# A decode kernel: the first weight load cut into 16 and 112 partitions

## The chip, the cores and the metric

The kernel runs on one core of one Trainium2 chip. The metric is the device time of the whole program in microseconds (us); lower is better.

## The reference

One decode step: a layernorm of x, attention over a cache of 32768 positions with 32 heads, and a SwiGLU feed-forward, both added to x.

```python
D = 640; Hq = Hkv = 32; Sk = 32768; Dh = 128; F = 1728          # all bf16, one token
xn = layernorm(x)
q = (xn @ wq).reshape(32, 128)                                   # wq: 640 x 4096, 5.2 MB
scores = einsum("hd,hkd->hk", q, k_cache) * Dh ** -0.5           # k_cache: 32 x 32768 x 128
o = einsum("hk,hkd->hd", softmax(scores), v_cache)               # v_cache: the same size
out = x + o.reshape(4096) @ wo + (silu(xn @ w_gate) * (xn @ w_up)) @ w_down
```

K and V are 537 of the 554 MB that are read.

## The kernel before

SBUF is the core's on-chip memory, which the kernel uses as 128 rows, called partitions. PE is the matrix engine, DVE the vector engine and ACT the scalar engine; SP only issues loads here. SBUF holds a ring of three slots of 64 KB per partition. The loads take the slots in the order wq, K of head 0, K of head 1, V of head 0, K of head 2 and so on; each waits until what its slot held has been used. They are all issued from SP, on one DMA queue. wq and x are issued at the very start of the program, ahead of the barrier that lets the engines begin.

```python
units = [("wq",)]
for h in range(H):
    units.append(("k", h))
    if h >= 1:
        units.append(("v", h - 1))
...
ring = sbt("ring", [128, SLOTS, CE], BF16)              # CE = 32768 elements
wq = flat[:, WQ_S * CE:WQ_S * CE + NCD * H * DH]        # 128 partitions x 20480 elements = 40 KB each
...
ahead(lambda: nc.sync.dma_start(wq, A_wq.rearrange("(p c) n -> p (c n)", c=NCD)).then_inc(s_wq, 16))
ahead(lambda: nc.scalar.dma_start(xrow, A_x[0, 0:1, :]).then_inc(s_x, 16))
...
# SP, for each unit in turn
if s in owner:
    e.wait_ge(*owner.pop(s))                            # the slot's last user is done
...
elif u[0] == "k":
    e.dma_start(ring[:, s, :], kv_src(A_k_cache, u[1], 0, NJ)).then_inc(s_slot[s], 16)
...
# PE: q = xn @ wq, after the layernorm and after wq has landed
t.wait_ge(s_a, 11)
t.wait_ge(s_wq, 16)
with t.Fori(0, NQB) as b:
    for c in range(NCD):
        mm = t.matmul(banks[:, bass.ds(b * 512, 512)], lhsT=xnb[:, c, :],
                      rhs=wq[:, bass.ds(b * 512 + c * H * DH, 512)], ...)
```

For each head DVE multiplies K by q, PE sums the products, ACT takes the exponentials, and PE multiplies by V.

Of the kernel before, what the change touches and what calls it, by code (L numbers as in the profile page):

```python
# [12 lines left out]
def bass_parallel_sum__gqa_block_cached__swiglu_ffn__decode_kernel(  # L13
# [18 lines left out]
    NCD = D // 128  # L32
# [47 lines left out]
    with ExitStack() as es:  # L80
# [3 lines left out]
        def sem(name):  # L84
            return es.enter_context(nc.semaphore(name))
# [34 lines left out]
        s_x, s_wq, s_out = sem("x"), sem("wq"), sem("o")  # L120
# [18 lines left out]
        wq = flat[:, WQ_S * CE:WQ_S * CE + NCD * H * DH]  # L139
# [7 lines left out]
        def ahead(start):  # L147

            at_start = nc.main_func.blocks[0]
            n = len(at_start.instructions)  # L150
            start()
            ins = list(at_start.instructions)
            new = ins[n:]
            drain = next(i for i, x in enumerate(ins)
                         if x.engine == new[0].engine and type(x).__name__ == "InstDrain")
            at_start.instructions = ins[:drain] + new + ins[drain:n]

        ahead(lambda: nc.sync.dma_start(wq, A_wq.rearrange("(p c) n -> p (c n)", c=NCD)).then_inc(s_wq, 16))
        ahead(lambda: nc.scalar.dma_start(xrow, A_x[0, 0:1, :]).then_inc(s_x, 16))
        block = es.enter_context(nc.Block(no_gpsimd_drain=True))  # L160
        f0 = FFN_S * CE
# [46 lines left out]
        with nc.psum_tensor("ps8", [128, 8, 512], F32) as ps8:  # L208
# [72 lines left out]
            def pe(t):  # L281
# [13 lines left out]
                t.matmul(misc[:, 1:2], lhsT=ones[:, :], rhs=st[:, 2:3], start=True, stop=True).then_inc(s_pa, 1)  # L295

                t.wait_ge(s_a, 11)
                t.wait_ge(s_wq, 16)
                with t.Fori(0, NQB) as b:
                    for c in range(NCD):  # L300
                        mm = t.matmul(banks[:, bass.ds(b * 512, 512)], lhsT=xnb[:, c, :],  # L301
# [373 lines left out]
```

## Time and profile before

| | before |
|---|---|
| time, median | 1286.4 us (1286.2 to 1286.6) |
| bytes moved, mean rate | 554 MB, 431 GB/s |
| DMA, PE, DVE busy | 99.8%, 81%, 52% |
| wq, from issue to landing | 15.0 us |
| first DVE multiply of head 0 starts | 34.5 us |

Lines of the profile's page before the change. The DMA and GB/s rows cut the span into 40 slices of 32 us; a 9 is a busy share of 90% or more of the 16 DMA engines. The last line sums the chain of work that ended last.

```profile
span 1284.8 us, 10032 instructions
...
DMA  9999999999999999999999999999999999999998
GB/s 424 424 453 425 426 427 445 428 433 441 431 433 426 445 428 433 439 433 426 433 445 428 431 431 441 428 433 445 428 431 426 445 428 433 439 433 431 428 429 368
DMA packets 10987, 554.16 MB, mean 431 GB/s; under 512 B 1247, under 2 KB 1504, under 8 KB 1760
...
q1 hardware_dynamic: 10974, 554.00, 99.8%
...
DMA 53%; PE 29%; DVE 11%; issue 6%; DVEq 0%; SPq 0%
```

The DMA engines have work in every slice, so the kernel is bound by its stream of loads.

The timeline of the kernel before (start, duration, engine, line, operation; in brackets the idle time before it and what ended it):

```profile
0.00 0.41 SPq L158 DMA_DIRECT2D ring<-in_A_wq_dram  x1
...
1.76 0.35 PE L286 MATMUL ps<-one,ring 1*128 1x1 bf16 x5 [1.76 <-DMA ring<-in_A_x_dram]
...
15.41 11.10 PE L301 MATMUL ps<-ring 128*128 x40 [10.60 <-DMA ring<-in_A_wq_dram]
...
34.50 17.43 DVE L577 TENSOR_TENSOR ring<-ring,qb 128x8192 bf16<-128x8192 bf16 x4 [27.80 <-DMA ring<-in_A_k_cache_dram]
```

wq is the first thing that PE needs after the layernorm: it waits 10.6 us for it. DVE then waits for K of head 0, the next load in the queue.

The DMA issues of the kernel before (times issued, KB if one size, median us from issue to landing):

```profile
ring<-in_A_wq_dram SPq DMA_DIRECT2D x1, 5120.0 KB, 15.0
...
ring<-in_A_k_cache_dram SPq DMA_DIRECT2D x32, 41.4
```

A K load takes 41.4 us from issue to landing, though 8.4 MB at 433 GB/s need 19.4 us: about two loads are queued at any time.

Windows of the kernel before; the last two columns are DMA share and GB/s (bytes are counted where a packet starts, so short windows are rough):

```profile
core 0: us, PE busy (x) PEld busy (x) DVE busy (x) ACT busy (x) POOL busy (x), PEclk, DMA share, GB/s
0.00:15.00 15.00, 1.66 (x14) 1.40 (x14) 2.55 (x13) 1.49 (x2) 2.61 (x18) 1.00 1.01 420
15.00:30.00 15.00, 11.10 (x40) 4.48 (x40) 0.00 (x0) 6.06 (x9) 0.00 (x0) 1.00 0.97 419
30.00:45.00 15.00, 5.93 (x17) 0.20 (x2) 10.50 (x3) 0.00 (x0) 0.00 (x0) 0.54 0.97 419
...
100.00:1200.00 1100.00, 908.89 (x4043) 210.39 (x2309) 596.41 (x345) 39.44 (x112) 0.00 (x0) 0.90 1.00 434
```

The trace also records each DMA packet. In wq's load a packet is one partition's 40 KB row. The records do not name the engine, but the packets follow one another in 16 chains of eight, one chain for each DMA engine. Sorted by start and taken in rounds of 16, their median durations in ns are:

```
kernel before: 2140 1514 1514 1514 1514 1514 1514 1514   last wq packet ends at 14.69 us
```

Apart from the start-up in the first, a packet takes 1.514 us: 27.05 GB/s per engine, 433 GB/s for 16. The first packet starts at 1.02 us. Each chain ends with one packet of 4 bytes, 16 in all, of 9 ns each: as many as the load adds to its semaphore, the completion writes.

### The profile page before, as it was taken

What the parts mean: (1) busy time and instruction counts of PE and PEld (TensorE: products, weight loads), DVE (VectorE), ACT (ScalarE), POOL (GpSimd) and SP (SyncE); (2) the same over time, 40 slices, a digit from 0 to 9 for tenths busy, and PEclk for the clock granted to TensorE, in tenths of its full rate; (3) what the DMA queues carried; (4) which work ended last, traced back from release to release, by engine and by line L of the source; (5) the groups of instructions that cost most, each with busy time, mean ns of one, the idle gap of its engine ahead of it and who ended that gap; (6) DMA issues with size and microseconds to landing.
All of it is one profiled execution on the core that took longest, in us unless ns stands there. A gap on an engine that the chain in (4) does not pass through costs nothing.

```text
span 1284.8 us, 10032 instructions
## 1 busy us (share of the span) xinstructions
PE 1043.2 (81%) x5160; PEld 261.3 (20%) x3240; DVE 672.2 (52%) x409; ACT 52.2 (4%) x139; POOL 2.6 (0%) x18
## 2 busy tenths in 40 slices
PE   3599777789777788778898887798788798778897
PEld 1021112221112221112221112221112221112227
DVE  0855665445664446664446664446654446654451
ACT  2000000000000000000000000000000000000000
POOL 0000000000000000000000000000000000000000
PEclk9799888898888999888998888998888998888995
DMA  9999999999999999999999999999999999999998
GB/s 424 424 453 425 426 427 445 428 433 441 431 433 426 445 428 433 439 433 426 433 445 428 431 431 441 428 433 445 428 431 426 445 428 433 439 433 431 428 429 368
DMA packets 10987, 554.16 MB, mean 431 GB/s; under 512 B 1247, under 2 KB 1504, under 8 KB 1760
## 3 DMA queue, kind: packets, MB, share of 16 engines
q1 hardware_dynamic: 10974, 554.00, 99.8%
q8 instruction: 9, 0.15, 0.0%
q14 instruction: 2, 0.02, 0.0%
q10 hardware_dynamic: 2, 0.00, 0.0%
HBM read 553.99 MB, written 0.00 MB: 431 GB/s over the span
## 4 chain that ended last, share of the span: by engine, by line
DMA 53%; PE 29%; DVE 11%; issue 6%; DVEq 0%; SPq 0%
DMA ring<-in_A_k_cache_dram 51%; PE ps L358 16%; DVE ring L577 11%; PE ps L310 10%; DMA ring<-in_A_wo_dram 2%; PE ps L342 1%; PE ps L329 1%; PE ps L400 0%; PE ps L394 0%; PE ps L388 0%; PE ps L451 0%; SPq L252 0%; DVEq L577 0%; DVE sc L583 0%; DVE pmax L589 0%
## 5 line engine op out<-in xcount | busy, mean ns | idle before, releaser
L577 DVE TENSOR_TENSOR ring<-ring,qb 128x8192 bf16<-128x8192 bf16 x128 | 557.8, 4420 | 314.8 <-DMA ring<-in_A_k_cache_dram 314.8
L310 PE MATMUL ps<-ring,ident 128*128 128x512 bf16 x1920 | 498.9, 419 | 0.0
L358 PE MATMUL ps<-ring,P 128*4 128x512 bf16 x1920 | 429.0, 379 | 0.0
L329 PE MATMUL ps<-ring,ident 128*128 128x512 bf16 x128 | 55.9, 437 | 218.7 <-DVE ring L577 218.2
L358 PEld LDWEIGHTS ps<-ring,P 128*4 128x4 bf16 x1920 | 158.1, 85 | 230.1
L329 PEld LDWEIGHTS ps<-ring,ident 128*128 128x128 bf16 x128 | 12.6, 99 | 616.9 <-issue 313.3
L583 DVE TENSOR_REDUCE sc<-ps 128x64 f32<-128x512 f32 x128 | 82.3, 684 | 63.8 <-PE ps L310 63.8
L595 DVE TENSOR_SCALAR negb<-ps 128x1 f32<-128x1 f32 x32 | 5.1, 159 | 108.4 <-PE ps L400 108.4
L503 ACT ACTIVATE P<-sc,negb 128x256 bf16<-128x256 f32 x32 | 16.2, 508 | 956.9 <-DVE negb L595 956.9
L592 DVE TENSOR_REDUCE m<-ps 1x1 f32<-1x128 f32 x32 | 8.9, 278 | 85.2 <-PE ps L394 85.2
L380 PEld LDWEIGHTS ps<-identf,o 4*128 4x128 f32 x248 | 30.7, 190 | 13.1 <-issue 13.1
L380 PE MATMUL ps<-identf,o 4*128 4x1 f32 x248 | 33.3, 251 | 0.0
L388 PEld LDWEIGHTS ps<-rsum,ones 128*128 128x128 f32 x64 | 12.1, 190 | 99.9 <-issue 99.1
L494 ACT ACTIVATE o<-ps,rzb 4x512 f32<-4x512 f32 x31 | 21.0, 678 | 6.3 <-PE ps L345 6.3
L301 PE MATMUL ps<-ring 128*128 x40 | 11.1, 448 | 10.6 <-DMA ring<-in_A_wq_dram 10.6
L499 ACT ACTIVATE ocol<-ps 128x1 f32 (+1 forms) x31 | 5.4, 174 | 222.3 <-PE ps L380 222.3
L342 PE MATMUL ps<-ring,P 128*4 x64 | 14.4, 379 | 0.0
L589 DVE TENSOR_REDUCE pmax<-sc 128x1 f32<-128x256 f32 x32 | 13.4, 420 | 0.0
L394 PE MATMUL ps<-identf,pmax 128*1 128x128 f32 x64 | 12.2, 272 | 1.2 <-DVE pmax L589 1.2
L400 PE MATMUL ps<-m,ones 1*128 1x1 f32 x64 | 12.1, 256 | 0.4 <-DVE m L592 0.4
L400 PEld LDWEIGHTS ps<-m,ones 1*128 1x128 f32 x64 | 9.4, 182 | 14.0 <-issue 13.3
L565 DVE RECIPROCAL rzb<-ps 128x1 f32<-128x1 f32 x32 | 5.1, 158 | 8.1 <-PE ps L388 8.1
(75 smaller groups left out, 97.4 us busy)
## 6 DMA issues: line engine op xcount, KB each, us to landing
ring<-in_A_v_cache_dram SPq DMA_DIRECT2D x2, 4096.0 KB, 36.3
ring<-in_A_wq_dram SPq DMA_DIRECT2D x1, 5120.0 KB, 15.0
ring<-in_A_wo_dram SPq DMA_DIRECT2D x3, 1280.0 KB, 24.2
ring<-in_B_w_gate_dram SPq DMA_DIRECT2D x1, 2160.0 KB, 22.6
ring<-in_B_w_up_dram SPq DMA_DIRECT2D x1, 2160.0 KB, 27.5
ring<-in_B_w_down_dram SPq DMA_DIRECT2D x1, 2080.0 KB, 30.9
ring<-in_A_wo_dram SPq DMA_DIRECT2D x1, 800.0 KB, 28.3
ring<-in_A_k_cache_dram SPq DMA_DIRECT2D x32, 41.4
```

The source lines that it names most:

```text
L310: return t.add_instruction(mybir.InstMatmult(start_tensor_calc=False, stop_tensor_calc=stop, tile_size=(128, 128), tile_position=(0, 0), l ...
L329: t.matmul(ob, lhsT=ident[:, :], rhs=src, start=True, stop=False)
L342: t.matmul(O, lhsT=P[:, h % PR, bass.ds(b * (RUN * W) + j, W)], rhs=flat[:, bass.ds(b * (RUN * W * DH) + (s * CE + j * DH), W * DH)], star ...
L358: mm = t.matmul(O, lhsT=P[:, h % PR, j:j + W], rhs=ring[:, s, j * DH:(j + W) * DH], start=(j == 0), stop=(j + W == NJ))
L380: mm = t.matmul(fold_ps, lhsT=o4[:, m * DH:(m + 1) * DH], rhs=identf[0:W, m:m + 1], start=(m == 0), stop=(m == W - 1))
L394: t.matmul(misc[0:1, 0:128], lhsT=pmax[:, h % SR:h % SR + 1], rhs=identf[:, :], start=True, stop=True).then_inc(s_t, 1)
L400: t.matmul(misc[:, 128:129], lhsT=ones[0:1, :], rhs=m1[0:1, h % SR:h % SR + 1], start=True, stop=True).then_inc(s_b, 1)
L494: a.activation(out=o4[:, :], in_=O, func=ACTF.Copy, scale=rzb[0:W, h % SR:h % SR + 1]).then_inc(s_o4, 1)
L503: a.activation(out=P[:, h % PR, :], in_=sc[:, :], func=ACTF.Exp, bias=negb[:, h % SR:h % SR + 1], scale=c_scale, accum_out=rsum[:, h % SR: ...
L577: v.tensor_tensor(out=kh, in0=kh, in1=q[:, None, :].to_broadcast([128, HF, DH]), op=ALU.mult).then_inc(s_mul, 1)
L583: v.tensor_reduce(out=sc[:, i * HF:(i + 1) * HF], in_=bank[i].rearrange("p (j e) -> p j e", e=G), axis=AX.X, op=ALU.add).then_inc(s_red, 1)
L589: v.tensor_reduce(out=pmax[:, h % SR:h % SR + 1], in_=sc[:, :], axis=AX.X, op=ALU.max).then_inc(s_max, 1)
```

## The change

The first load is cut in two, 16 partitions (one 40 KB packet for each of the 16 chains) and then the other 112. The natural intent is that a small first load is set up sooner, so that the engines start sooner. Both loads count on the same semaphore, and PE waits for both.

```diff
-        ahead(lambda: nc.sync.dma_start(wq, A_wq.rearrange("(p c) n -> p (c n)", c=NCD)).then_inc(s_wq, 16))
+        wq_src = A_wq.rearrange("(p c) n -> p (c n)", c=NCD)
+        for a, b in ((0, 16), (16, 128)):
+            ahead(lambda: nc.sync.dma_start(wq[a:b, :], wq_src[a:b, :]).then_inc(s_wq, 16))
...
-                t.wait_ge(s_wq, 16)
+                t.wait_ge(s_wq, 32)
```

## The prediction

> **What bounds the kernel now.** The stream of loads. The page gives 554.16 MB at a mean of 431 GB/s over a span of 1284.8 us, the DMA row shows 9 in every slice until the last, and queue 1's packets fill 99.8% of the 16 engines' time. The chain of waits is mostly K-cache loads (51%), and PE or DVE work in it overlaps queued transfers: a K load takes a median 41.4 us from issue to landing, about two 8 MB transfers (19.3 us each at 433 GB/s), so the queue is never empty. Hence whatever delays the slowest DMA engine at the start comes back nearly 1:1 in the total.
>
> **The start, from the timeline and DMA windows.** wq's issue takes 0.41 us on SP; the first bytes move at about 1.0 us; wq (128 rows of 40 KB, eight per engine) lands 15.0 us after issue. The layernorm chain is done at 6.7 us, so the q matmuls wait 10.6 us for wq. They end near 26.5 us; K of head 0 lands at 34.4 us, so wq may land some 8 us later before q delays the first DVE multiply.
>
> **What the change does.** Same bytes, same queue. It adds one issue (0.41 us on SP, hidden: 5 MB are queued behind it) and 16 completion writes (nanoseconds each). The intended gain is an earlier first byte. The small x load, issued at 0.12 us, also starts moving near 1.0 us (0.9 us later), so at most 0.1-0.2 us can be gained: 0.01%.
>
> **The possible cost.** [...] The present trace, with 128-partition loads only, can't tell. [...] I worked an estimate [...] from 27 GB/s per engine (433/16) and contiguous groups of seven: wq lands near 23-26 us instead of 15, fast engines running ahead into K, and the slowest engine ends 10 us late. That delay persists to the end.
>
> If the 112 were dealt round robin[...]: about +36 us (estimate, same sharing). [...]
>
> **Predicted time:** 1295 us, that is +8.5 us (0.7%); 8 in 10 between 1286 and 1300. Chances: faster by over 2% 0.01, within 2% 0.89, slower by over 2% 0.10.
>
> **What would show each step.**
> - First byte still near 1.0 us (windows at the start).
> - Crowding: GB/s in the first slice of the page falls from 424 while the DMA share stays at 9; the wq issues' time to landing rises to 23-26 us; the first DVE multiply starts near 44 us rather than 34.5.
> - From the third slice on, GB/s as before (425-453), and per-head spacing unchanged at some 38.7 us; all the difference lies before 50 us and shifts everything after.
>
> **What would make it wrong.** [...] Round robin dealing: then 1322. A lag that is partly recovered because engines end unequal and the last transfers even them out: then +3 to +6 us.

The forecast's sum came to 1295 us: 1286.4 of the kernel before and 8.5 for the change. 23 to 26 us for wq, 10 us for the slowest engine and +36 us (1322) for dealing round robin were estimates. The completion writes that it names took 9 ns each in the trace before, and 13 to 41 ns each for the two loads of the change.

## The result

The changed kernel took 1298.78 us (median of four, 1298.68 to 1299.03) against 1286.36 us: 12.4 us or 1.0% slower. The ratio is 1.0097 (95% interval 1.0079 to 1.0114); ratios are the mean time of one kernel's fast runs over that of the other's of the same rounds, so not quite the ratio of the medians quoted.

The page after the change:

```profile
span 1297.3 us, 10033 instructions
...
DMA  9999999999999999999999999999999999999998
GB/s 259 449 423 437 433 427 439 428 441 428 430 438 428 445 424 430 438 428 445 428 430 436 432 438 428 436 432 430 438 428 438 430 430 438 428 441 428 430 428 362
DMA packets 11004, 554.17 MB, mean 427 GB/s; under 512 B 1263, under 2 KB 1520, under 8 KB 1776
...
q1 hardware_dynamic: 10990, 554.00, 99.7%
...
DMA 53%; PE 28%; DVE 12%; issue 6%; DVEq 0%; SPq 0%
```

The first slice fell from 424 to 259 GB/s while the DMA row stayed at 9: the engines are as busy as before and move less. 165 GB/s less over 32.4 us (1297.3 / 40) is 5.3 MB, which at 431 GB/s is 12.4 us: the whole loss stands in that one slice. From the third slice on the rates are those of before.

The timeline after:

```profile
0.00 0.86 SPq L160 DMA_DIRECT2D ring<-in_A_wq_dram  x2
...
2.82 0.35 PE L288 MATMUL ps<-one,ring 1*128 1x1 bf16 x5 [2.82 <-DMA ring<-in_A_x_dram]
...
27.87 11.01 PE L303 MATMUL ps<-ring 128*128 x40 [22.00 <-DMA ring<-in_A_wq_dram]
...
46.97 17.43 DVE L579 TENSOR_TENSOR ring<-ring,qb 128x8192 bf16<-128x8192 bf16 x4 [39.21 <-DMA ring<-in_A_k_cache_dram]
```

q's matmuls start 12.46 us later (27.87 against 15.41), the first DVE multiply 12.47 us later (46.97 against 34.50). The layernorm started about 1 us later too, behind the x load (2.82 against 1.76), without effect: PE still waited 22 us for wq.

The issues and windows after:

```profile
ring<-in_A_wq_dram SPq DMA_DIRECT2D x1, 4480.0 KB, 27.0
...
ring<-in_A_wq_dram SPq DMA_DIRECT2D x1, 640.0 KB, 8.8
ring<-in_A_k_cache_dram SPq DMA_DIRECT2D x32, 41.5
```

```profile
core 0: us, PE busy (x) PEld busy (x) DVE busy (x) ACT busy (x) POOL busy (x), PEclk, DMA share, GB/s
0.00:15.00 15.00, 1.66 (x14) 1.41 (x14) 2.55 (x13) 1.49 (x2) 2.59 (x18) 1.00 1.02 205
15.00:30.00 15.00, 2.13 (x6) 0.84 (x7) 0.00 (x0) 0.00 (x0) 0.00 (x0) 1.00 0.94 285
30.00:45.00 15.00, 8.88 (x36) 3.60 (x34) 0.00 (x0) 6.06 (x9) 0.00 (x0) 0.92 1.03 446
...
100.00:1200.00 1100.00, 902.05 (x4031) 211.71 (x2327) 593.55 (x339) 40.30 (x115) 0.00 (x0) 0.90 1.00 434
```

The 16 partitions took 8.8 us to land; the 112 took 27.0. Between 100 and 1200 us both kernels move 434 GB/s, and the median K or V packet takes 2.422 us in both. The packets of wq, as above:

```
kernel after: 4810 3790 2884 2180 2368 2573 2785 2630   last wq packet ends at 26.73 us
```

No packet of the changed load took less than 1.84 us, where nearly all took 1.51 before. The last one ends 12.0 us later, which is nearly all of the 12.4 us. The first packet starts at 1.03 us, so the intended gain is not there at all.

### The profile page after: what moved, and what is told of

It reads as the page before. It is cut to its first block, busy times and chain, and to the rows that moved or that the text cites. A ratio compares the mean times of both kernels' runs of the same rounds, so it can differ in the third digit from the quotient of the medians.

```text
span 1297.3 us, 10033 instructions
## 1 busy us (share of the span) xinstructions
PE 1038.6 (80%) x5160; PEld 261.3 (20%) x3240; DVE 672.2 (52%) x409; ACT 52.1 (4%) x139; POOL 2.6 (0%) x18
## 4 chain that ended last, share of the span: by engine, by line
DMA 53%; PE 28%; DVE 12%; issue 6%; DVEq 0%; SPq 0%
DMA ring<-in_A_k_cache_dram 51%; PE ps L360 16%; DVE ring L579 12%; PE ps L312 9%; DMA ring<-in_A_wo_dram 2%; PE ps L344 1%; PE ps L331 1%; PE ps L402 0%; PE ps L396 0%; PE ps L390 0%; PE ps L453 0%; SPq L254 0%; DVEq L579 0%; DVE sc L585 0%; DVE pmax L591 0%
## 5 line engine op out<-in xcount | busy, mean ns | idle before, releaser
L312 PE MATMUL ps<-ring,ident 128*128 128x512 bf16 x1920 | 493.0, 415 | 0.0
L331 PE MATMUL ps<-ring,ident 128*128 128x512 bf16 x128 | 56.0, 438 | 222.8 <-DVE ring L579 222.2
L303 PEld LDWEIGHTS ps<-ring 128*128 128x128 bf16 x40 | 4.4, 111 | 28.2 <-issue 24.9
```

Of the source, the lines that this page charges most:

```text
L312: return t.add_instruction(mybir.InstMatmult(start_tensor_calc=False, stop_tensor_calc=stop, tile_size=(128, 128), tile_position=(0, 0), l ...
L331: t.matmul(ob, lhsT=ident[:, :], rhs=src, start=True, stop=False)
```

## The experiments

The theory under test: how fast a load runs depends on which SBUF partitions it writes at the same time; the expectations of e9 and e11 call it crowding. Rivals: A, a second load costs time in itself; B, the source rows, neighbours in HBM, are slow to read together; C, any load of fewer than 128 partitions is slow. D and E were added for e9 to e12, where they are told.

The expectations had a picture of where engines meet. No trace or run shows it. A number after a mark that names no rival is the theory's; the totals of e2 to e7 that it gives (+36, +12 and +8 to +12 us) were estimates and rested on that picture. What the runs show is how long the packets took for each set of partitions.

Unless stated, an experiment is the kernel before with another split of wq, and PE waits for all of its loads. e1 was timed in rounds; the others are one run each, set against the kernel before on the same chip (e2 to e4 against the seven runs of e1's rounds, the rest against one; all 1286.2 to 1286.6).

### e1: cut by columns instead of partitions

```diff
+        for a, b in ((0, 2560), (2560, 20480)):
+            ahead(lambda: nc.sync.dma_start(wq[:, a:b], wq_src[:, a:b]).then_inc(s_wq, 16))
```

> wq again in two loads, the first again 1/8 of the bytes, but cut by columns: both loads cover all 128 partitions (5 KB and 35 KB per row). [...] no loss, 1286.4 us +-0.5, wq lands about 15 us after issue. Rival A (a second load, its issue and its completion writes cost the time): as the change, near 1298.8 us.

Measured: 1286.35 us against 1286.29, ratio 1.000 (0.998 to 1.002), wq waited for as long as before. From the page and the list of waits:

```profile
DMA  9999999999999999999999999999999999999998
GB/s 424 424 449 427 426 433 441 428 433 441 430 428 430 445 426 433 439 435 426 433 445 426 433 433 441 426 433 445 426 428 433 443 428 433 441 430 428 430 427 371
```

```profile
PE ps L303 <- DMA ring<-in_A_wq_dram: 10.5, 1, 10.5
```

The same number of loads and the same sizes, without any loss: rival A falls. There is no gain either; the first packet again starts at 1.02 us. A smaller first load did not start the engines sooner.

### e2 to e5: eight loads of 16 partitions, destination and source set apart

```diff
+        for j in range(8):
+            ahead(lambda: nc.sync.dma_start(DST, SRC).then_inc(s_wq, 16))
# e2: DST = wq[16*j:16*j+16, :]   SRC = wq_src[16*j:16*j+16, :]
# e3: DST = wq[j:128:8, :]        SRC = wq_src[j:128:8, :]
# e4: DST = wq[16*j:16*j+16, :]   SRC = wq_src[j:128:8, :]
# e5: DST = wq[j:128:8, :]        SRC = wq_src[16*j:16*j+16, :]
```

> wq in eight loads of 16 neighbouring partitions (0-15, 16-31, ...), right result. [...] wq lands near 48-50 us, total about +36 us (1322). Rival A (cost per added load): 7 added loads, 7 times +12.4 us if each costs the same. Rival B (the source rows, neighbours in HBM, are slow to read together): also large, so this run needs e4 beside it.

> wq in eight loads of 16 partitions each, every eighth one (j, j+8, ..., j+120), source rows the same, right result. [...] wq lands near 24-26 us, total about +12 us (1298). Rival A: the same as e2_blocks, having as many loads. Rival B: no loss if only neighbouring rows are slow.

> Eight loads into neighbouring partitions as in e2_blocks, but reading every eighth row as in e3_strided; the result is wrong on purpose, rows of wq are in other partitions. [...] (destination decides): as e2_blocks, about +36 us. Rival B (source decides): as e3_strided.

> Eight loads into every eighth partition as in e3_strided, but reading neighbouring rows as in e2_blocks; the result is wrong on purpose. [...] (destination decides): as e3_strided, about +12 us. Rival B (source rows decide): as e2_blocks.

| | destination | source rows | time, us | against before | median packet after the first, us |
|---|---|---|---|---|---|
| e2 | 16 neighbours | neighbours | 1319.71 | +33.4 | 5.74 |
| e4 | 16 neighbours | every eighth | 1319.25 | +33.0 | 5.61 |
| e3 | every eighth | every eighth | 1300.34 | +14.1 | 3.17 |
| e5 | every eighth | neighbours | 1299.66 | +13.2 | 3.18 |

PE's wait for wq, from the lists of waits of e2, e4, e3 and e5 in that order (total, times, longest):

```profile
PE ps L303 <- DMA ring<-in_A_wq_dram: 40.6, 1, 40.6
```

```profile
PE ps L303 <- DMA ring<-in_A_wq_dram: 40.0, 1, 40.0
```

```profile
PE ps L303 <- DMA ring<-in_A_wq_dram: 19.9, 1, 19.9
```

```profile
PE ps L303 <- DMA ring<-in_A_wq_dram: 19.1, 1, 19.1
```

The destination decides and the source changes nothing beyond 1 us: rival B falls. All four have eight loads, so their number is not it either. Sixteen rows, 655,360 bytes, take 5.74 us into 16 neighbouring partitions (114 GB/s), 3.17 us into every eighth (207 GB/s) and 1.514 us in the load of all 128 (433 GB/s). The author's estimates of +36 and +12 us came out as +33 and +13 to +14. (e4 and e5 put rows of wq into wrong partitions. The comparison with the reference passed all the same, so it does not feel such an error; that the other splits are right rests on each partition getting its own row.)

### e6 and e8: 64 partitions, at the edge or in the middle

```diff
+        for a, b in ((0, 64), (64, 128)):                  # e6
+        for a, b in ((32, 96), (0, 32), (96, 128)):        # e8
+            ahead(lambda: nc.sync.dma_start(wq[a:b, :], wq_src[a:b, :]).then_inc(s_wq, 16))
```

> wq in two loads of 64 partitions (0-63, 64-127), right result. [...] wq lands near 25 us, total about +12 us (1298). Rival A (a second load costs): also near +12 us. Rival C (only loads of 16 partitions or a number that is no multiple of 32 lose): no loss, 1286.4 us.

> wq in three loads: partitions 32-95, then 0-31, then 96-127; right result. [...] 32-95 are as many partitions as a half[...]: its packets take 1.51 us like those of the unsplit load (3.2 us in a half); 0-31 and 96-127[...] their two packets per engine take 3.2 us. Sum: 4 times 1.7 us, total about +6.8 us (1293). Rival C (any load of less than 128 partitions loses): as the halves, +13.5 us.

e6 took 1299.93 us (+13.5), e8 1293.82 us (+7.5). Median packets by round, in ns, and PE's wait for wq in e6, then in e8:

```
e6: 3073 3200 3200 3200 3001 3200 3198 3198
e8: 2190 1514 1514 1514 2812 3192 2983 3192
```

```profile
PE ps L303 <- DMA ring<-in_A_wq_dram: 23.4, 1, 23.4
```

```profile
PE ps L303 <- DMA ring<-in_A_wq_dram: 17.3, 1, 17.3
```

Partitions 32-95 load as fast as all 128 (1.514 us per packet), partitions 0-63 at a little under half that rate. The sizes are equal; what differs is which 64 partitions they are. Rival C falls, and so does the narrower form of it in e6's expectation (that only numbers which are no multiple of 32 lose). This is the clearest evidence that the choice of partitions decides: an innocent-looking cut into halves costs 13.5 us, and a load half as wide as the whole costs nothing if it lies right (e8's 7.5 us come from the two edge loads after it, whose packets took 2.8 to 3.2 us). e8 also came within 0.7 us of the sum that was written down for it.

### e7: the 112 first

```diff
+        for a, b in ((16, 128), (0, 16)):
```

> The change with its two loads in the other order, 112 partitions first, then 16; right result. [...] the 112 land about 3-5 us later than at full rate[...]; wq lands near 21-25 us, total +8 to +12 us. If the loss of the 112 in the change was only the after-effect of the 16 ahead of them (engines out of step), the 112 land here at about 12 us and the total is +5 us or less.

It took 1298.87 us (+12.4), with wq's rounds at 2742 2723 2291 2095 2717 2736 2657 4848 ns, the 16 partitions now in the last. The 112 are slow in their own right, not as an after-effect of the 16 ahead of them. The total lies just above the range expected, but one step of the expectation missed: the 112 were to land 3 to 5 us later than the 12 us of the full rate, and landed at 23.2 us. That was the first sign that the estimate's sharing does not describe them.

### e9 to e11: one extra load to chosen partitions

Why all packets of the 112 are slow was still unexplained. Rival D: an engine is slow at partitions that another engine writes in a load of 128. Rival E: where some engines crowd, all are held up. A probe of one 22 KB row per engine was put between wq and K, into 16 partitions: 32 to 92 in steps of four (e10, the control), 11 to 116 in steps of seven (e9, for D) and 0 to 105 in steps of seven (e11, for E). That e9 and e11 meet the conditions of D and E was the assumption; which engine writes which partition the traces do not record.

```diff
+        spare = flat[:, x0 + NCD * 128 + D:WQ_S * CE + CE]
+        ahead(lambda: nc.sync.dma_start(spare[PARTS, :], extra).then_inc(s_extra, 16))
# SP, before V of head 0 takes the slot: e.wait_ge(s_extra, 16)
# e9: PARTS = 11:117:7    e10: PARTS = 32:96:4    e11: PARTS = 0:106:7
```

> The kernel before plus one extra load between wq and K, one row of 22 KB into each of 16 partitions (11, 18, ..., 116), into space that nothing else uses; right result. [...] Crowding theory: 0.81 us per packet as at full rate, total +0.8 us. Rival D[...]: 1.1 us or more per packet, total +1.1 us or more.

> As e9, but partitions 32, 36, ..., 92[...]. Both theories: 0.81 us per packet, total +0.8 us; it is the control of e9 and e11.

> As e9, but partitions 0, 7, ..., 105[...]. Crowding theory[...]: four packets take 1.7 us, twelve 0.81 us; total +1.7 us for the slowest engine. Rival E[...]: all 16 packets take about 1.2 us or more, total above +1.2 us.

| | partitions | time, us | the 16 probe packets, us: least, median, most | median of the K packets just after, us |
|---|---|---|---|---|
| e10 | 32, 36, ..., 92 | 1287.37 | 0.818, 0.818, 0.818 | 2.418 |
| e9 | 11, 18, ..., 116 | 1288.29 | 0.868, 0.893, 1.161 | 2.704 |
| e11 | 0, 7, ..., 105 | 1288.35 | 0.976, 1.249, 1.445 | 2.869 |

e10 is the clean control: 22,016 bytes in 0.818 us are 26.9 GB/s per engine, the full rate. e9 fits neither expectation in full: its total, 1.95 us above the kernel before, is in the range that rival D named, but its packets are 9% slower in the median, and only one of the 16 reached the 1.1 us that D asked of all. So D in the size that could explain the 112 is unlikely, though not excluded; and the K packets after the probe are slower too. The engines do not start the probe together (13.8 to 15.6 us), so it overlaps with the last of wq and the first of K; what that does was not tested by itself. The trace has one more hint: 15 of the 16 probe packets had ended by 15.4 us and only one engine, a late one, still wrote its probe until 16.8 us, and yet the first K packets of all 16 engines took 2.59 to 3.37 us, against 2.418 in e10. That fits rival E. In e11 the theory without E expected twelve packets of 0.81 us, yet not one of the 16 came near 0.82 us; E asked for about 1.2 us of all, and the least took 0.976. That is nearer to E, though whatever slowed e9 may be mixed in, and the number of twelve rested on the picture. The totals of e9 and e11 do not tell the two layouts apart; the packets do.

### e12: the 112 dealt by hand

```diff
+        for ps in [slice(0, 16)] + [slice(16 + r, 122 + r, 7) for r in range(7)]:
+            ahead(lambda: nc.sync.dma_start(wq[ps, :], wq_src[ps, :]).then_inc(s_wq, 16))
```

> Partitions 0-15 first as in the change, then the other 112 in seven loads of 16: r, r+7, ..., r+105 for r = 16 to 22, so that each engine gets seven neighbouring partitions in order, if a 16-partition load gives one to each engine in order; right result. If the 112-partition load deals them the same way (seven neighbours per engine)[...]: the packets of each round take what they took in the change (about 3.7, 2.9, 2.2, 2.4, 2.5, 2.8, 2.7 us) and the total is 1298.8 +-0.7. If the 112 are dealt another way: another pattern[...].

It took 1298.65 us (+12.4). The rounds beside those of the changed kernel:

```
after: 4810 3790 2884 2180 2368 2573 2785 2630
e12:   4848 3617 2883 2243 2359 2607 2887 2748
```

The pattern is the same to within 0.18 us per round. So the load of 112 behaves as if each engine takes seven neighbouring partitions in order, if a load of 16 gives one to each. No packet of e12 took less than 1.99 us, where an undisturbed one takes 1.51, while the estimate behind the prediction had fast engines running ahead. Rival E would give that. It is inferred and not isolated: no run has one slow engine and all others at partitions that were fast by themselves, and a loss of D's kind that is larger in this load than in e9 is not excluded. Through which path the engines are held up is not shown by any run.

## Why the prediction was right or wrong

- **The bound, and that a delay at the start comes back in full: right.** The last wq packet is 12.04 us late, and the first K packet of the engine that ends last took 2.63 us instead of 2.42. That is 12.25 of the 12.4 us; the rest was not traced. Rates after the second slice are unchanged.
- **No gain from an earlier first byte: right.** 1.03 us against 1.02; e1 shows the same (1.02 us) where both loads cover all partitions.
- **The partitions that a load covers as the cause: right**, and now shown: by destination (e2 to e5), by position at equal width (e6, e8), and not by the number of loads (e1). Why those partitions are slow together no run shows, and how it slows the load of 112, about half of the loss, is in part inferred (see e12).
- **The first load:** The first two rounds, over which the engines even out (their ends lie 1.8 us apart after the first, 0.9 after the second), lost 2.67 and 2.28 us in the median, 4.95 together.
- **The 112: mis-sized.** The failing term is "fast engines running ahead into K". The other six rounds took 15.42 us (sum of the medians after) instead of 9.08, a loss of 6.3: the engines finished wq between 24.63 and 26.73 us, close together, none running far ahead, and no packet took less than 1.84 us. So the estimate for the slowest engine, 10 us, came out at 12.
- **The number: low.** 1295 had been set below even that estimate; the prediction does not say why, but it lists a case in which only 3 to 6 us are lost. The measured time lies inside the range, near its upper end, and that says little by itself, since the range reaches from no loss at all to 1300; the loss is 1.46 times the predicted one (12.4 over 8.5).
- **The signs:** first slice down with DMA at 9, right; wq landing predicted at 23 to 26 us, measured 27.0; first DVE multiply predicted near 44 us, measured 47.0, both late by the same mis-sized term. Dealing round robin (estimated at +36 us) is what e2 does by hand, +33; the load of 112 did not behave so: the medians of its rounds were 2.18 to 2.88 us, not 5.74.

## What to carry to other kernels

When a load is cut, look at which partitions each piece covers, not only at its bytes: cut by columns and keep all 128 partitions (e1, no loss), or choose partitions like 32-95, which loaded at the full rate here (1.514 us per packet). Spreading 16 rows widely was not enough in e9 (0.893 us per packet against 0.818 in e10). A DMA share near 100% did not mean full speed: the first slice showed a 9 at 424 GB/s before and a 9 at 259 after. Read it with the GB/s, and read packet durations where the two disagree. In this kernel, whose load queue never runs dry, the 12.0 us lost in the first load were lost for good (+12.4 us in the total). No version here beat the kernel before: with the first packet of wq at 1.02 us before and at 1.02 to 1.42 us in every other run, the cut had nothing to gain.
